# Respreading the loads, features and DMA transposes of each attention batch in a fused cosformer-attention and FFN kernel

## The chip, the cores and the metric

The kernel runs on one core of one Trainium2 chip. Its time is the device time of one execution in microseconds (us). A trace starts and ends with the first and last instruction, so its span is some 2 us shorter than the time. Runs count as slow when they are over 1.5% above the fastest of the same kernel.

## The reference

```python
B, H, S, D = 8, 8, 576, 64
def phi(x, c, s):                       # c, s: cos and sin of pi/2 * pos / S
    r = np.maximum(x, 0.0)
    return np.concatenate([r * c, r * s], axis=-1)
q_p, k_p = phi(q, cos_w, sin_w), phi(k, cos_w, sin_w)
kv  = einsum('bhsf,bhsd->bhfd', k_p, v);  z = sum(k_p, axis=2)
num = einsum('bhsf,bhfd->bhsd', q_p, kv); den = einsum('bhsf,bhf->bhs', q_p, z)[..., None] + 1e-6
x = (num / den).transpose(0, 2, 1, 3).reshape(B * S, H * D)     # 4608 tokens x 512
out = (((x @ w1) * (x @ w2)) @ w3) @ w_out
```

## The kernel before

TensorE runs a fixed program. The FFN works on 9 tiles of 512 tokens. It is cut into 232 steps: tile 0 has 40, each later tile 24, so tile t starts at step 16 + 24 t. A step is mostly four 512-column matmuls. The attention of a batch is cut into small calls hung on chosen steps. They are loads of k, v and q in two pieces each, five key features (`kf`), five value copies (`vc`), five kv products (`kv`), five query features each with its DMA transpose (`qf`), and five products, each normalized and transposed into the FFN's input xT (`nu`).

```python
def features(b, dst, src, c, cos=True, sin=True, scalar_heads=H):
    ...                                                   # cut
    nc.vector.tensor_scalar(out=dst[:R, c, :, 0:D], in0=src[:R, :, c, :], ...)           # cos half
    n = scalar_heads
    nc.scalar.activation(out=dst[:R, c, 0:n, D:F], in_=src[:R, 0:n, c, :], func=ACTF.Relu, ...)  # sin half
    if n < H:
        nc.vector.tensor_scalar(out=dst[:R, c, n:H, D:F], in0=src[:R, n:H, c, :], ...)

def prep_q(b, c):
    features(b, feat_of(b)[1], raw[b, "q"], c, scalar_heads=H if b < 3 else 6)
    if c in dma_q(b):
        nc.sync.dma_start_transpose(out=att_of(b)["qpT"][...], in_=feat[b][1][...])

def x_tr(b, c, by_vector=False):
    ...                                                   # cut
    if b >= 2 or (b == 1 and c == 3):
        nc.sync.dma_start_transpose(out=xT[t][:, :, ds(o, R)], in_=xf[rows])
        return
    ...                                                   # cut: transposes on TensorE

def plan_loads(b, when):                                  # hold_back() ties a load to its step
    for piece, s in zip([(n, half) for n in "kvq" for half in range(2)], when):
        ...                                               # cut: at(s, hold_back and load)

bases = [75, 102, 127, 153, 178]                          # steps of each batch's first product
for b, last, base in zip(range(4, B), bases, bases[1:]):
    plan_loads(b, [last + s for s in (7, 9, 11, 12, 14, 16)])
    plan(b, kf=[last + s for s in (15, 16, 17, 18, 19)],
         vc=[last + s for s in (17, 18, 19, 20, 21)],
         kv=[base + s for s in (-3, -2, -2, -1, -1)],
         qf=[last + s for s in (20, 21, 22, 23, 24)],
         nu=[base + s for s in (0, 2, 4, 6, 8)])
```

## Time and profile before

| | before |
|---|---|
| time, median | 272.53 us (271.57 to 274.71, 3 runs) |
| span of the profiled run | 269.0 us |
| TensorE busy | 245.3 us, 91% |
| TensorE waiting after 70 us | 12.4 us in six rows of the list of waits |

The page's table of 40 equal slices shows where the losses lie. A digit is the busy share, or for PEclk the granted TensorE clock, in tenths.

```profile
PE   8789999999999999979999859997999399999993
...
PEclk9999999999999999999999979999999979999998
```

TensorE is dense for the first 17 slices, up to about 114 us. Then come four dips (7, 85, 7 and 3), one for each of the batches 4 to 7. Two of them are followed by a lower clock.

### The profile page before, as it was taken

What the parts mean: (1) busy time and instruction counts of PE and PEld (TensorE: products, weight loads), DVE (VectorE), ACT (ScalarE), POOL (GpSimd) and SP (SyncE); (2) the same over time, 40 slices, a digit from 0 to 9 for tenths busy, and PEclk for the clock granted to TensorE, in tenths of its full rate; (3) what the DMA queues carried; (4) which work ended last, traced back from release to release, by engine and by line L of the source; (5) the groups of instructions that cost most, each with busy time, mean ns of one, the idle gap of its engine ahead of it and who ended that gap; (6) DMA issues with size and microseconds to landing.
All of it is one profiled execution on the core that took longest, in us unless ns stands there. A gap on an engine that the chain in (4) does not pass through costs nothing.

```text
span 269.0 us, 5058 instructions
## 1 busy us (share of the span) xinstructions
PE 245.3 (91%) x1837; PEld 131.5 (49%) x1867; DVE 145.9 (54%) x380; ACT 125.5 (47%) x270; POOL 93.5 (35%) x197
## 2 busy tenths in 40 slices
PE   8789999999999999979999859997999399999993
PEld 3487555556854454434544425444545144444442
DVE  6875735555876567238645735357556536322420
ACT  2765317766734752337335613356345513324321
POOL 7564320250423500524044404441264100969200
PEclk9999999999999999999999979999999979999998
DMA  7999999799869984995889884996799753798515
GB/s 193 185 194 203 208 208 198 100 116 145 136 107 167 140 131 78 172 181 86 156 149 166 121 160 97 171 161 116 153 147 191 81 108 72 191 309 263 182 29 127
DMA packets 83896, 41.02 MB, mean 152 GB/s; under 512 B 51488, under 2 KB 80416, under 8 KB 83872
## 3 DMA queue, kind: packets, MB, share of 16 engines
q0 software_dynamic: 35456, 27.20, 65.4%
q1 hardware_dynamic: 48256, 13.38, 29.7%
q8 instruction: 14, 0.23, 0.4%
q10 hardware_dynamic: 160, 0.13, 0.2%
q14 instruction: 10, 0.08, 0.1%
HBM read 38.80 MB, written 9.44 MB: 179 GB/s over the span
## 4 chain that ended last, share of the span: by engine, by line
PE 55%; DMA 30%; ACT 4%; issue 4%; POOL 3%; DVE 3%; ACTq 0%; POOLq 0%
PE ffnps L432 23%; PE ffnps L486 21%; DMA qs<-in_q_dram 14%; DMA w3b<-in_moe_w_dram 6%; DMA qpT<-qp 4%; PE pnum L349 4%; PE ffnps L226 3%; DMA w2b<-in_moe_w_dram 3%; DMA ks<-in_k_dram 2%; ACT asb L469 2%; ACT qp L263 1%; PE pnum L291 1%; DVE xblk L361 1%; PE pst L214 1%; DVE kvs L297 1%
## 5 line engine op out<-in xcount | busy, mean ns | idle before, releaser
L432 PE MATMUL ffnps<-xT,w2b 128*128 128x512 bf16 (+2 forms) x329 | 74.3, 348 | 2.1 <-DVE abT L473 1.8
L432 PE MATMUL ffnps<-xT,w1b 128*128 128x512 bf16 (+2 forms) x326 | 74.0, 347 | 1.4 <-ACT asb L469 0.5
L486 PE MATMUL ffnps<-w34b,abT 128*128 128x512 bf16 x270 | 68.7, 393 | 2.9 <-DVE abT L473 1.4
L473 DVE TENSOR_TENSOR abT<-asb,ffnps 128x512 bf16<-128x512 bf16 x64 | 43.7, 683 | 41.7 <-PE ffnps L432 40.0
L469 ACT CAST asb<-ffnps 128x512 bf16<-128x512 f32 x64 | 37.0, 579 | 45.2 <-PE ffnps L432 38.8
L521 POOL COPY seen<-mark 1x1 bf16<-1x1 bf16 x52 | 9.3, 179 | 112.9 <-ACT mark L519 112.9
L432 PEld LDWEIGHTS <-w1b 128*128 128x128 bf16 x336 | 31.0, 98 | 29.3 <-issue 1.6
L493 ACT COPY osb<-ffnps 128x512 f32<-128x512 f32 x35 | 20.5, 585 | 53.0 <-PE ffnps L486 47.5
L432 PEld LDWEIGHTS <-w2b 128*128 128x128 bf16 x336 | 30.6, 98 | 29.0 <-issue 2.4
L486 PEld LDWEIGHTS <-abT 128*128 128x128 bf16 x280 | 26.1, 100 | 30.9 <-issue 4.3
L263 ACT ACTIVATE qp<-qs,sinv 128x384 bf16<-128x384 bf16 (+4 forms) x40 | 24.6, 648 | 10.9 <-DMA qs<-in_q_dram 6.2
L361 DVE TENSOR_TENSOR xblk<-pnum,den 128x512 bf16<-128x512 f32 (+1 forms) x39 | 26.9, 691 | 1.6 <-DVE den L360 0.2
L263 ACT ACTIVATE kp<-ks,sinv 128x384 bf16<-128x384 bf16 (+3 forms) x35 | 21.7, 641 | 8.3 <-DMA ks<-in_k_dram 8.3
L349 PE MATMUL pnum<-kvs,qpT 128*128 128x65 bf16 x312 | 16.7, 195 | 8.9 <-DMA qpT<-qp 7.5
L349 PEld LDWEIGHTS <-qpT 128*128 128x128 bf16 x320 | 15.0, 99 | 19.8 <-issue 7.8
L283 POOL COPY va<-vs 128x512 bf16<-128x512 bf16 (+1 forms) x30 | 17.6, 627 | 17.4 <-DMA vs<-in_v_dram 12.7
L417 POOL DMA_DIRECT2D out_dram<-osb x42 | 22.3, 535 | 2.6 <-issue 2.5
L359 DVE TENSOR_SCALAR den<-pnum 128x8 f32<-128x8 f32 (+1 forms) x39 | 6.4, 165 | 26.8 <-PE pnum L349 26.7
L259 DVE TENSOR_SCALAR qp<-qs,cosv 128x512 bf16<-128x512 bf16 (+1 forms) x40 | 15.1, 387 | 7.3 <-DMA qs<-in_q_dram 7.2
L259 DVE TENSOR_SCALAR kp<-ks,cosv 128x512 bf16<-128x512 bf16 (+1 forms) x35 | 13.3, 384 | 10.0 <-DMA ks<-in_k_dram 9.9
L226 PE MATMUL ffnps<-woutb,w3T 128*128 128x512 bf16 x62 | 14.9, 379 | 0.1
L291 PEld LDWEIGHTS <-kp 128*128 128x128 bf16 x280 | 11.5, 98 | 4.4 <-PE ffnps L432 0.3
(84 smaller groups left out, 194.2 us busy)
## 6 DMA issues: line engine op xcount, KB each, us to landing
out_dram<-osb POOLq DMA_DIRECT2D x16, 256.0 KB, 4.2
out_dram<-osb POOLq DMA_DIRECT2D x24, 128.0 KB, 3.6
qs<-in_q_dram POOLq DMA_DIRECT2D x9, 256.0 KB, 6.5
ks<-in_k_dram POOLq DMA_DIRECT2D x7, 320.0 KB, 6.3
qs<-in_q_dram POOLq DMA_DIRECT2D x7, 320.0 KB, 7.7
vs<-in_v_dram POOLq DMA_DIRECT2D x7, 320.0 KB, 7.3
ks<-in_k_dram POOLq DMA_DIRECT2D x7, 256.0 KB, 6.4
vs<-in_v_dram POOLq DMA_DIRECT2D x7, 256.0 KB, 7.5
```

The lines of the kernel that those rows point to most:

```text
L226: nc.tensor.matmul(acc[:, :], lhsT=w3T[:, lc, :], rhs=woutb[:, lc, :], start=(lc == 0), stop=(lc == 7))
L259: nc.vector.tensor_scalar(out=dst[:R, c, :, 0:D], in0=src[:R, :, c, :], scalar1=0.0, scalar2=cosv[:R, at:at + 1], op0=ALU.max, op1=ALU.mult)
L263: nc.scalar.activation(out=dst[:R, c, 0:n, D:F], in_=src[:R, 0:n, c, :], func=ACTF.Relu, scale=sinv[:R, at:at + 1], bias=0.0)
L283: eng.tensor_copy(out=feat_of(b)[2][:R, c, :, 0:D], in_=raw[b, "v"][:R, :, c, :])
L349: nc.tensor.matmul(nt[:, h // 4, ds((h % 4) * 65, 65)], lhsT=qpT[:, h, ds(at, 128)], rhs=kvs[:, h, :], start=True, stop=True)
L361: nc.vector.tensor_tensor(out=xblk[rows], in0=n4[:, :, :, 0:D], in1=den[rows].unsqueeze(3).to_broadcast([R, 2, 4, D]), op=ALU.mult)
L417: on.dma_start(out=rows[:, :, cols], in_=osb[64 * i:64 * i + rows.shape[0], :, cols])
L432: nc.tensor.matmul(out, lhsT=w[:, kc, ts(jc, 128)], rhs=x[:, kc, tok], start=(kc == 0), stop=(kc == 3))
L469: nc.scalar.copy(out=asb[:], in_=aT[:, :])
L473: nc.vector.tensor_mul(out=abT[:, jc, :], in0=asb[:], in1=bT[:, :])
L486: nc.tensor.matmul(ops[:, :], lhsT=abT[:, jc, ts(ms, 128)], rhs=w34b[:, jc, :], start=(jc == 0), stop=(jc == 7))
L493: nc.scalar.copy(out=osb[:, ms % 2, :], in_=ops[:, :])
```

## The change

The intent is to use the whole cycle of a batch, about 25 steps. Loads of keys and queries go at least 9 steps ahead of their features. Query features and their transposes go 12 steps ahead of the product. Loads, features and products sit 2 to 4 steps apart, mostly 3 or 4. The order of loads becomes k, q, v, and the sin half of every feature runs whole on ScalarE.

```diff
     def prep_k(b, c):
-        features(b, feat_of(b)[0], raw[b, "k"], c, scalar_heads=H if b < 3 else 6)
+        features(b, feat_of(b)[0], raw[b, "k"], c)
     def prep_q(b, c):
-        features(b, feat_of(b)[1], raw[b, "q"], c, scalar_heads=H if b < 3 else 6)
+        features(b, feat_of(b)[1], raw[b, "q"], c)
 ...
-        for piece, s in zip([(n, half) for n in "kvq" for half in range(2)], when):
+        for piece, s in zip([(n, half) for n in "kqv" for half in range(2)], when):
 ...
-    plan_loads(3, (51, 53, 55, 57, 59, 61))
-    plan(3, kf=(59, 60, 62, 63, 65), vc=(62, 63, 64, 65, 66), kv=(72, 73, 73, 74, 74),
-         qf=(67, 69, 71, 73, 75), nu=(75, 77, 79, 81, 83))
-    bases = [75, 102, 127, 153, 178]
+    plan_loads(3, (46, 48, 51, 53, 56, 59))
+    plan(3, kf=(54, 57, 59, 61, 63), vc=(64, 65, 66, 67, 68), kv=(71, 72, 72, 73, 73),
+         qf=(60, 63, 66, 69, 72), nu=(74, 77, 80, 84, 87))
+    bases = [74, 101, 126, 152, 176]
     for b, last, base in zip(range(4, B), bases, bases[1:]):
-        plan_loads(b, [last + s for s in (7, 9, 11, 12, 14, 16)])
-        plan(b, kf=[last + s for s in (15, 16, 17, 18, 19)],
-             vc=[last + s for s in (17, 18, 19, 20, 21)],
+        plan_loads(b, [last + s for s in (-8, -5, -1, 3, 7, 11)])
+        plan(b, kf=[last + s for s in (4, 7, 10, 13, 15)],
+             vc=[base + s for s in (-10, -9, -8, -7, -6)],
              kv=[base + s for s in (-3, -2, -2, -1, -1)],
-             qf=[last + s for s in (20, 21, 22, 23, 24)],
-             nu=[base + s for s in (0, 2, 4, 6, 8)])
+             qf=[base + s for s in (-12, -9, -6, -3, 0)],
+             nu=[base + s for s in (0, 3, 6, 9, 12)])
 ...   # cut: the same loads of batch 2 in the new order; output stores some steps moved
```

More of the change, by code (lines that the diff above doesn't have):

```diff
@@ L590 @@
         at(s, lambda c=c: q_tr(1, c))
-    plan_loads(2, (27, 28, 35, 36, 31, 33))
+    plan_loads(2, (27, 28, 31, 33, 35, 36))
     plan(2, kf=(33, 35, 37, 39, 40), vc=(41, 42, 43, 44, 45), kv=(45, 46, 46, 47, 47),
          qf=(40, 41, 42, 43, 44), nu=(48, 50, 52, 54, 57))
-    plan_loads(3, (51, 53, 55, 57, 59, 61))
-    plan(3, kf=(59, 60, 62, 63, 65), vc=(62, 63, 64, 65, 66), kv=(72, 73, 73, 74, 74),
-         qf=(67, 69, 71, 73, 75), nu=(75, 77, 79, 81, 83))
-    bases = [75, 102, 127, 153, 178]
+    plan_loads(3, (46, 48, 51, 53, 56, 59))
+    plan(3, kf=(54, 57, 59, 61, 63), vc=(64, 65, 66, 67, 68), kv=(71, 72, 72, 73, 73),
+         qf=(60, 63, 66, 69, 72), nu=(74, 77, 80, 84, 87))
+    bases = [74, 101, 126, 152, 176]
     for b, last, base in zip(range(4, B), bases, bases[1:]):
-        plan_loads(b, [last + s for s in (7, 9, 11, 12, 14, 16)])
-        plan(b, kf=[last + s for s in (15, 16, 17, 18, 19)],
-             vc=[last + s for s in (17, 18, 19, 20, 21)],
+        plan_loads(b, [last + s for s in (-8, -5, -1, 3, 7, 11)])
+        plan(b, kf=[last + s for s in (4, 7, 10, 13, 15)],
+             vc=[base + s for s in (-10, -9, -8, -7, -6)],
              kv=[base + s for s in (-3, -2, -2, -1, -1)],
-             qf=[last + s for s in (20, 21, 22, 23, 24)],
-             nu=[base + s for s in (0, 2, 4, 6, 8)])
+             qf=[base + s for s in (-12, -9, -6, -3, 0)],
+             nu=[base + s for s in (0, 3, 6, 9, 12)])
     for i in range(2 * (NT - 1)):
@@ L611, in put @@
             store(nc.gpsimd, kept[i][:, :, :], 2 * i, 2)
-        at((81, 107, 132, 158)[i] if i < 4 else max(189 + 2 * (i - 4), 40 + 12 * (i - 2)), put)
+        at((88, 115, 140, 166)[i] if i < 4 else 185 + 2 * (i - 4), put)
     g = 0
```

## The prediction

> **What bounds the kernel now.** I first read the page's engine totals. TensorE is busy 245.3 of 269.0 us, VectorE 54%, ScalarE 47%. So the end can come earlier only where TensorE stands still or runs slowly. Then I asked whom TensorE's matmuls waited for, from 70 us (the second FFN tile; the change touches nothing before it) to the end.
>
> ```profile
> PE pnum L349 <- DMA qpT<-qp: 7.5, 3, 3.6
> PE ffnps L432 <- DVE abT L473: 1.8, 1, 1.8
> PE ffnps L486 <- DVE abT L473: 1.4, 1, 1.4
> PE ffnps L486 <- ACT asb L469: 0.9, 1, 0.9
> PE ffnps L432 <- ACT asb L469: 0.5, 1, 0.5
> ```
>
> Columns: us in all, times, longest. With one more row of 0.3 us (the first product waiting for the copy of kv) that is 12.4 us. The largest row is the first attention product of a batch (L349), waiting for the DMA transposes of its query features. The rows on abT and asb look like FFN evictions, but the timeline around 119 us shows what those really waited for:
>
> ```profile
> 119.04 0.61 ACT L263 ACTIVATE kp<-ks,sinv 128x384 bf16<-128x384 bf16 x1 [3.49 <-DMA ks<-in_k_dram]
> ...
> 119.47 0.68 DVE L473 TENSOR_TENSOR abT<-asb,ffnps 128x512 bf16<-128x512 bf16 x1
> ...
> 120.21 1.02 PE L432 MATMUL ffnps<-xT,w2b 128*128 128x512 bf16 x4 [1.82 <-DVE abT L473]
> ```
>
> The key features of batch 4 head the queues of ScalarE and VectorE, their load has not landed, both engines stand still (in brackets: 3.49 us on ScalarE, and 4.18 us on VectorE in a row left out), the FFN evictions behind them stand too, and TensorE runs out of PSUM tiles. So all these waits have one cause: loads are issued a few us ahead of their features, and transposes a few us ahead of their product. The chain of work that ended last agrees (start, us, what):
>
> ```profile
> 200.34 8.21 DMA qs<-in_q_dram
> 208.68 0.42 issue
> 209.10 0.47 ACT asb L469
> 209.57 1.31 ACT qp L263 x3
> 210.89 4.93 DMA qpT<-qp
> 215.87 0.62 PE pnum L349 x8
> 216.49 3.15 PE ffnps L486 x8
> 219.64 0.26 PE pnum L349 x8
> 219.90 1.73 PE ffnps L486 x8
> ```
>
> A query load takes 8.21 us, its features follow at once, their transpose takes 4.93 us and only then comes the product. The last lines show a second cost: eight output matmuls take 3.15 us right after the stall and 1.73 us later, so 1.42 us more. After the 3.56 us stall of batch 5 the same eight take 3.41 us, 1.68 more.
>
> The stretches between the first products of successive batches (3 to 4, 4 to 5, 5 to 6, 6 to 7; last 2 to 3, a well-fed cycle for comparison):
>
> ```profile
> 100.19:129.64 29.45, 26.62 (x184) 12.99 (x188) 17.52 (x48) 13.54 (x32) 8.84 (x19) 1.00 0.84 135
> 129.64:157.51 27.87, 24.10 (x176) 12.28 (x180) 16.45 (x45) 13.19 (x31) 8.86 (x19) 1.00 0.98 146
> 157.51:186.37 28.86, 27.14 (x182) 13.13 (x185) 15.57 (x44) 13.23 (x31) 10.32 (x22) 0.94 0.87 136
> 186.37:215.87 29.50, 24.47 (x177) 12.24 (x181) 16.36 (x44) 12.98 (x31) 9.37 (x20) 1.00 1.08 145
> ...
> 74.09:100.19 26.10, 25.88 (x186) 13.10 (x188) 16.55 (x44) 14.08 (x31) 8.20 (x17) 1.00 0.99 134
> ```
>
> After the window come its length, then busy us of PE, PEld, DVE, ACT, POOL, the granted clock, DMA share and GB/s. The cycle up to batch 3 (last line) is 27 program steps long (first products at steps 48 and 75) and takes 26.10 us with TensorE busy 99%. The four later ones are 27, 25, 26 and 25 steps and take 28 to 29.5 us.
>
> **What the Trainium skill says.** "TensorE: Matmul & The Clock Gate", section "Part 1: The HAM clock gate", says that TensorE falls to half clock after about 3.4 us idle and returns after a busy window as long. The trace agrees: the stalls of 3.56 and 3.41 us are followed by matmuls at about twice the time, and that of 0.53 us (batch 6) by none. So a long stall here costs about 1.5 us more than its length. The same page's specification table calls the queues of ScalarE and VectorE strict FIFO; the quoted 119 us timeline agrees. "DMA: Bandwidth & Descriptors", section "Issuing engines are not separate DMA queues", says that DMAs of all issuers share the same 16 engines and interleave. The trace agrees at least for crowding: five pieces of batch 4, issued 1 to 2 us apart, take 7.6 to 9.1 us from issue to landing, those of batch 3, 2 steps apart, 5.3 to 7.0. "Perfetto Trace Analysis", section "Identifying the Most-Contended Engine", warns that DMA occupancy misleads and that HBM use should be read: here 179 GB/s over the span.
>
> **The change, part by part.** One step is one FFN group: four 512-column matmuls, 4 x 0.216 = 0.864 us (the chain has eight in 1.73).
>
> Loads. For batches 4 to 7 the key pieces move from 7 and 9 steps after the previous batch's first product to 8 and 5 before it; their features come 4 to 15 after. That is at least 9 steps, over 8 us, from second piece to first feature, against 6 before. Queries load at -1 and 3, and their features start 12 steps before the batch's own first product, 12 to 15 after the previous one. So at least 9 steps there too. A load of 5.3 to 7.0 us is then hidden. This removes the abT and asb waits, 4.6 us.
>
> Transposes. Each chunk's transpose is now issued 12 steps ahead of its product, over 10 us, against 3.3 us from issue to landing (page, 32 transposes). The built program's waits show that the first product waits only for the transposes of its own columns (one, or two in odd batches), not for the one just issued. This removes 7.5 us and with it both slow stretches, 1.42 + 1.68 = 3.1 us.
>
> Features. Every second half of a feature now runs whole on ScalarE: 50 activations grow from 384 to 512 columns, 613 to 721 ns, so +5.4 us of ScalarE, and 50 VectorE operations of 0.25 to 0.38 us go (7.3 + 7.1 less the first batch's 0.3, 14 us). ScalarE has 13 us of work in a 29 us cycle; neither is on the path once the data is there. I count 0.
>
> Product spacing goes from 2 to 3 steps; normalizing one takes 0.18 + 0.21 + 0.70 us, inside 2 steps already. 0.
>
> Sum in two ways. By waits: 12.4 + 3.1 = 15.5 us. By pace: batch 3's cycle gives 26.10 us for 27 steps, so 24.37 for 25 and 25.24 for 26; losses 29.45 - 26.10 = 3.35, 27.87 - 24.37 = 3.50, 28.86 - 25.24 = 3.62, 29.50 - 24.37 = 5.13, sum 15.6 (this includes batch 5's slow stretch), plus the tail's 1.42: 17.0 us. The pace also counts gaps too short for the list of waits; I take it. Full success: 272.5 - 17.0 = 255.5 us.
>
> **Rivals.** *GpSimd's value copies become the late link.* Values now load last, second piece at 11 steps after the previous first product, and kv products start 21 to 24 after it. Landing in 7.0 us (7.2 steps of 0.967 us), plus 0.5 us of mark and issue, puts the data at about step 18.7; four copies of 0.63 us and, on the same queue, the next key load with its mark (1.1 us) end at 22.4. The last kv products come at step 23 to 26, and batch 7, with only 23, has no next key load. A margin of 1 to 3 steps; at 9.1 us landing, the worst piece seen, it would be gone in some batches and cost about 0.5 us each, at most 2 in all. I charge 1.5 us for this and other small new waits. *DMA becomes the bound.* A cycle moves about 135 GB/s x 29.45 us = 4.0 MB; in 25 us that is 160 GB/s. Five-us stretches of loads with transposes reach 195 to 202, the tail's stores 305, so I estimate enough room, and 10 us of lead absorbs slower transposes. Were each cycle held at 27 us by it, the gain would halve: about 264. *Transposes are slower among loads*, so that products still wait; speaking for it, those of x take 5.1 to 6.7 us in crowded stretches against 3.3 alone. Even 6.7 fits in 10. *ScalarE's longer features delay the FFN evictions*: 0.1 us each against a rotation of four PSUM tiles; under 1 us in all.
>
> **Range and chances.** 255.5 + 1.5 = 257.0 us. Below: everything hidden and a run like the fastest of before (271.57), 254 and a little less. Above: half of the gain lost to DMA crowding, 264. Range 253 to 263. 2% faster is 267.1 us; to miss it two thirds of the stalls would have to come back. Faster 0.95, same 0.04, slower 0.01.
>
> **What would show it.** In the changed profile: no wait of L349 for qpT over 0.5 us; ScalarE and VectorE hardly wait for ks and qs (before 14.5 and 17.1 us, a small part of it in the unchanged start); the four cycles at 0.97 to 1.0 us per step; granted clock near 1.00 after 70 us; the chain almost only matmuls from 100 us on, no DMA of qs. What would make it wrong: kv products (L291) waiting for GpSimd's va; load landings over 9 us everywhere and feature waits of the old size; or a PSUM wait on evictions behind the longer activations.

## The result, and the profile after

The changed kernel took 259.33 us (median; 257.85 to 262.3 in 4 runs, of which the one at 262.3 counts as slow) beside 272.84 us for the kernel before (4 runs). The ratio of the fast runs is 0.948, 95% interval 0.940 to 0.957. Ratios here are the mean time of one kernel's fast runs over that of the other's of the same rounds, so they are not quite the ratio of the medians. The span went from 269.0 to 256.0 us.

The waits of TensorE's matmuls from 70 us on (us in all, times, longest), which were six rows and 12.4 us before, are now two rows:

```profile
PE ffnps L432 <- DMA xT<-xblk: 2.8, 2, 1.5
PE ffnps L432 <- ACT osb L493: 0.9, 1, 0.9
```

All the old waits are gone: qpT, abT, asb and the copy of kv. A wait stands there that the list of before did not have after 70 us. The first matmul of an FFN tile waits for a DMA transpose of the attention output; the two of the first row are tile 2 at 89.8 us and tile 6 at 186.0 us. The second row is the same case: it is the first matmul of tile 5, at 161.06 us, the last transpose that it needs landed at 160.96 us, and in a repeat of this kernel that place is listed as a wait for xT.

The cycles, from first product to first product, in the columns of the prediction's table (window, length, busy us of PE, PEld, DVE, ACT, POOL, then clock, DMA share, GB/s):

```profile
74.16:100.78 26.62, 25.18 (x182) 12.67 (x185) 14.75 (x35) 14.71 (x33) 9.05 (x20) 1.00 1.39 149
100.78:126.87 26.09, 25.82 (x185) 13.12 (x189) 15.05 (x35) 14.95 (x32) 8.78 (x19) 1.00 1.25 159
126.87:151.23 24.36, 24.14 (x177) 12.32 (x180) 15.32 (x36) 13.42 (x31) 8.69 (x19) 1.00 1.19 162
151.23:177.49 26.26, 25.13 (x181) 12.80 (x185) 14.39 (x36) 15.04 (x32) 10.20 (x22) 1.00 1.14 151
177.49:202.71 25.22, 23.45 (x173) 11.86 (x176) 15.01 (x35) 13.88 (x28) 7.41 (x15) 1.00 1.12 158
```

The first line is the cycle of 26 steps up to batch 3. It held 27 steps before, and took 26.10 us then. The next four hold 27, 25, 26 and 24 steps. They took 29.45, 27.87, 28.86 and 29.50 us for 27, 25, 26 and 25 steps. Two things can be read here. The cycles to batches 4 and 5 run at 0.97 us per step, the pace that was foretold for all. The other three lost 1 us or more each: TensorE is busy only 25.18 of 26.62 us in the first line, for instance. The clock is 1.00 everywhere.

The chain of work that ended last, from 179 us on (start, us, what), answers to the chain of before:

```profile
179.10 6.86 DMA xT<-xblk
186.01 1.90 PE ffnps L432 x8
187.91 0.26 PE pnum L349 x8
188.17 2.59 PE ffnps L432 x12
...
202.71 0.42 PE pnum L349 x8
203.13 2.59 PE ffnps L486 x12
```

No load and no qpT is in it any more. The first product of batch 7 (202.71) follows other TensorE work and the copy of kv without a stall, and the matmuls behind it run at full speed (12 in 2.59 us). What is left in this stretch is a transpose of x that took 6.86 us.

Why are transposes of x late? The list of DMA issues gives medians from issue to landing. Before:

```profile
qpT<-qp SPq DMA_TRANSPOSE x32, 3.3
xT<-xblk SPq DMA_TRANSPOSE x31, 3.2
```

After:

```profile
qpT<-qp SPq DMA_TRANSPOSE x32, 5.1
xT<-xblk SPq DMA_TRANSPOSE x31, 4.7
```

The same transposes take half as long again now that more loads run beside them, the longest of x 10.4 us in place of 7.4. That loads are the cause is tested by run 9 below.

### The profile page after: what moved, and what is told of

The parts are those of the page before. It is cut to its first block, busy times and chain, and to the rows that moved or that the text cites. A ratio compares the mean times of both kernels' runs of the same rounds, so it can differ in the third digit from the quotient of the medians.

```text
span 256.0 us, 5013 instructions
## 1 busy us (share of the span) xinstructions
PE 241.5 (94%) x1837; PEld 131.3 (51%) x1867; DVE 137.6 (54%) x330; ACT 131.2 (51%) x270; POOL 92.8 (36%) x197
## 4 chain that ended last, share of the span: by engine, by line
PE 80%; DMA 10%; DVE 3%; ACT 3%; issue 2%; POOL 1%; ACTq 0%; POOLq 0%
PE ffnps L432 46%; PE ffnps L486 17%; DMA xT<-xblk 7%; PE ffnps L226 5%; PE pnum L349 4%; PE pnum L291 3%; DMA qs<-in_q_dram 3%; PE pst L214 1%; DVE kvs L297 1%; DVE xblk L361 1%; PE pst L322 1%; ACT kvs L296 1%; PE pst L387 1%; ACT osb L493 0%; POOL vs L125 0%
## 5 line engine op out<-in xcount | busy, mean ns | idle before, releaser
L486 PE MATMUL ffnps<-w34b,abT 128*128 128x512 bf16 x270 | 64.1, 379 | 0.5
L263 ACT ACTIVATE qp<-qs,sinv 128x512 bf16<-128x512 bf16 (+2 forms) x40 | 28.0, 715 | 1.7 <-DMA qs<-in_q_dram 1.7
L263 ACT ACTIVATE kp<-ks,sinv 128x512 bf16<-128x512 bf16 (+1 forms) x35 | 24.9, 718 | 0.6 <-DMA ks<-in_k_dram 0.5
L259 DVE TENSOR_SCALAR qp<-qs,cosv 128x512 bf16<-128x512 bf16 (+1 forms) x40 | 17.7, 453 | 3.5 <-DMA qs<-in_q_dram 3.4
L291 PEld LDWEIGHTS <-kp 128*128 128x128 bf16 x280 | 11.5, 98 | 4.1
L291 PE MATMUL pnum<-va,kp 128*128 128x65 bf16 x280 | 12.2, 194 | 0.0
## 6 DMA issues: line engine op xcount, KB each, us to landing
out_dram<-osb POOLq DMA_DIRECT2D x16, 256.0 KB, 5.1
qs<-in_q_dram POOLq DMA_DIRECT2D x9, 256.0 KB, 8.4
ks<-in_k_dram POOLq DMA_DIRECT2D x7, 256.0 KB, 7.7
vs<-in_v_dram POOLq DMA_DIRECT2D x7, 256.0 KB, 4.7
```

Source lines behind the costliest of these rows:

```text
L291: nc.tensor.matmul(kvt[:, h // 4, ds((h % 4) * 65, 65)], lhsT=kp[:, c, h, :], rhs=va[:, c, h, 0:D + 1], start=(i == 0 and h % 4 == 0), sto ...
L486: nc.tensor.matmul(ops[:, :], lhsT=abT[:, jc, ts(ms, 128)], rhs=w34b[:, jc, :], start=(jc == 0), stop=(jc == 7))
```

## The experiments

Twelve more runs were made, one of them (e10) the changed kernel again. All gave correct results. My theory was at first that the lead of the loads is nearly all of the gain.

**1. Early loads alone (e3).** The kernel before, with only the loads moved.

```diff
-        plan_loads(b, [last + s for s in (7, 9, 11, 12, 14, 16)])      # order k, v, q
+        plan_loads(b, [last + s for s in (-4, -2, 0, 3, 7, 11)])       # order k, q, v
```

> The kernel before with one part of the change alone: for batches 4 to 7 the loads are issued at steps -4, -2 (keys), 0, 3 (queries), 7, 11 (values) after the previous first product; all features, transposes and products stay bunched at the old steps. Theory (the late loads cause nearly everything; transposes then start at their planned 5 to 7 steps before the product and need about 3.3 to 5 us): no wait of the product for qpT over 0.7 us, abT and asb waits gone, clock near 1.00, time 256 to 261 us. Rival (the transposes' own 12 steps of lead are needed): waits for qpT stay at 1 to 3 us per batch, time 264 to 269 us.

Measured: 289.12 us (287.73 to 290.7, all fast), ratio 1.0625, interval 1.055 to 1.070. Both the theory and the rival fell. The early loads alone make the kernel 6% slower. TensorE's waits in this run, from 95 us on:

```profile
PE pnum L349 <- DMA qpT<-qp: 15.3, 8, 4.5
PE ffnps L432 <- DMA xT<-xblk: 8.7, 2, 5.6
```

The waits on abT and asb are gone, as foretold, so loads no longer hold up the features. But the transposes are now the stall. The chain of this run shows how long single ones take:

```profile
101.33 8.30 DMA qpT<-qp
...
132.67 11.54 DMA xT<-xblk
144.21 0.14 issue
144.34 12.76 PE ffnps L432 x52
```

In the kernel before, the transposes of batches 4 to 7 lie from 7 steps before the first product to 8 after it, and loads are issued 7 to 16 steps after it. Most transposes meet no load. Those of x that do are slow there too: four of batch 2's five, beside the loads of batch 3, took 6.5 to 7.4 us. Early loads lie on top of the transposes, which start only 5 to 7 steps before the first product. So the two parts of the change can't be added up: the loads' lead costs 17 us without the transposes' lead.

**2. The rest that the first needed (e9).** The same kernel, with the query features and their transposes 12 to 8 steps ahead as well.

```diff
-             qf=[last + s for s in (20, 21, 22, 23, 24)],
+             qf=[base + s for s in (-12, -11, -10, -9, -8)],
```

> The kernel with early loads alone (289.1 us) plus one more part of the change for batches 4 to 7: query features and their transposes 12 to 8 steps before the first product, one step apart; x transposes still 2 steps apart, key features and the feature split still old. Theory formed after that run (early loads lie on top of the transposes, which then land in 5 to 11 us; only their 12 steps of lead make that harmless): the 15.3 us of waits for qpT and the slow matmuls after them go, waits for xT of a few us may remain, 262 to 270 us. Rival (the early loads harm in another way, for example by the order of the queue of GpSimd or by key loads at -4 and -2): still over 278 us.

Measured: 262.16 us (258.79 to 266.55), ratio of the two fast runs 0.952, interval 0.946 to 0.958. That is 27 us less than run 1, by this line alone. In the profiled run TensorE waits for qpT once, 0.9 us. So the revised theory holds: early loads and early transposes together make the gain. The key features are still bunched here, the products still 2 steps apart and the feature split still the old one; the output stores and the first products, which the change moves by some steps, stand at their old steps too. Yet the two fast runs (258.79 and 258.96 us) stand where the whole change stands. The other two runs, at 265 and 267 us, count as slow; I come back to this spread.

**3. Query features late again (e4).** The whole change, with `qf` moved back.

```diff
-             qf=[base + s for s in (-12, -9, -6, -3, 0)],
+             qf=[base + s for s in (-5, -4, -3, -2, -1)],
```

> The changed kernel with the query features and their transposes of batches 4 to 7 moved back to 5 to 1 steps before the first product (loads stay early). Theory (load lead is what counts): within 2 us of the changed kernel, about 258 to 261 us, waits for qpT at most 0.5 us per batch. Rival (transpose lead counts): a wait of 1.5 to 3.5 us before each of the four first products, 264 to 270 us.

Measured: 265.41 us median, but one run at 260.47 and three at 264.7 to 267.9, which leaves one fast run. The profile is of the fast one:

```profile
PE pnum L349 <- DMA qpT<-qp: 4.1, 3, 1.9
```

The waits of the product for qpT come back, though smaller than in run 1. The sign is the rival's: the transposes' lead matters. By the rule of 2% the verdict is unclear, and the size stays open between 1 and 9 us, since only the fast run has a profile.

**4. Bunched, with the leads kept (e5).** Is it the spacing of 3 to 4 steps that helps?

```diff
-        plan(b, kf=[last + s for s in (4, 7, 10, 13, 15)],
+        plan(b, kf=[last + s for s in (4, 5, 6, 7, 8)],
-             qf=[base + s for s in (-12, -9, -6, -3, 0)],
-             nu=[base + s for s in (0, 3, 6, 9, 12)])
+             qf=[base + s for s in (-12, -11, -10, -9, -8)],
+             nu=[base + s for s in (0, 2, 4, 6, 8)])
```

> The changed kernel with its leads kept but its spacing taken away for batches 4 to 7: key features at last+4 to +8 and query features with transposes at base-12 to base-8, one step apart, products 2 steps apart. Theory (lead, not spacing): within 1.5 us of the changed kernel, 257 to 260 us; perhaps faster where the x transposes come earlier. Rival (spacing keeps the queues of ScalarE and VectorE free for evictions): abT and asb waits of 1 us or more per batch, over 263 us.

Measured: 257.23 us (255.42 to 258.67, all fast), ratio 0.945, interval 0.938 to 0.952. Without the spacing of features and products the kernel is as fast, if anything faster. It is the lead that pays and not this spreading. The loads kept their spacing here; in run 9 four of the six stand 2 steps apart, and nothing is lost. Waits for xT in the profile of this run are one of 0.3 us. Tile 5's last block is produced one step earlier here. Tile 6's comes at the same step as in the change, and its transpose took 5.9 us in place of 6.9; no run shows why.

**5. Filling two stalls (e7).** The kernel before, with useless work on TensorE where it stood before the first products of batches 5 and 7.

```diff
+        if b in (5, 7):
+            at(base, lambda: filler(48))      # 48 transposes of zeros into a spare PSUM tile
```

> The kernel before with 48 useless 128-column transposes (about 2.7 us) put on TensorE just before the first products of batches 5 and 7, where it stood 3.4 to 3.6 us. Theory (the idle stretch itself throws the clock down afterwards): the stalls get no longer, the eight output matmuls after them take 1.73 us in place of 3.41 and 3.15, time about 3 us less, 269 to 270 us. Rival (the slow matmuls have another cause, or only queue behind something): same time as before or up to 3 us longer, 272 to 275 us.

Measured: 267.54 us (266.81 to 267.84), ratio 0.983, interval 0.977 to 0.988 (below 2%, so by rule unclear, but clear of 1): more work, and 4.4 us less. The chain after the first filler (start, us, what):

```profile
156.74 0.42 PE pnum L349 x8
157.16 1.73 PE ffnps L486 x8
158.89 0.26 PE pnum L349 x8
159.14 1.73 PE ffnps L486 x8
```

The first eight matmuls after the product take 1.73 us, where the same place took 3.41 us before; those after the second filler are as fast. The mean granted clock is 0.99 to 1.00 in place of 0.98. So it is the standing still that makes the following matmuls slow: with TensorE kept at work in the same place they are fast. This accounts for 3.1 us; where the other 1.3 us comes from I did not find.

**6 and 7. The feature split (e1, e2).** First the change without it, then it alone.

```diff
-        features(b, feat_of(b)[0], raw[b, "k"], c)                                          # e1; q alike
+        features(b, feat_of(b)[0], raw[b, "k"], c, scalar_heads=H if b < 3 else 6)
```

> The changed kernel with the old split of the feature halves (6 heads on ScalarE, 2 on VectorE from batch 3 on). Theory (neither engine is on the path once the data is there): 0 within 1 us, 258 to 260 us; ScalarE busy about 5 us less, VectorE about 12 us more. Rival (relief of VectorE was a part of the gain): 2 us or more slower, over 261 us.

Measured: 262.21 us median, two fast runs (257.68 and 261.3) and four between 261.9 and 262.8 that count as slow; ratio 0.954, interval 0.947 to 0.962. The profile that I have is of a slow run and shows 5.1 us of waits for xT, 3.7 us of them at tile 5, with a granted clock of 0.50 for the 3.4 us from then on. About the split this was inconclusive.

```diff
-        features(b, feat_of(b)[0], raw[b, "k"], c, scalar_heads=H if b < 3 else 6)          # e2; q alike
+        features(b, feat_of(b)[0], raw[b, "k"], c)
```

> The kernel before with only the split of the feature halves changed (all 8 heads on ScalarE). Theory: same within 1.5 us, 271 to 274 us, because features there wait for loads and not for the engines; late features get 0.1 us longer each, so if anything slightly slower. Rival (relief of VectorE): 268 to 270 us.

Measured: 271.31 us (270.52 to 272.4), ratio 0.998, interval 0.993 to 1.003. Alone, the split does nothing.

**8. Two blocks of x transposed on TensorE (e6).**

```diff
-        if b >= 2 or (b == 1 and c == 3):
+        if (b >= 2 and (b, c) not in ((3, 1), (6, 0))) or (b == 1 and c == 3):      # both 2 steps later
```

> The changed kernel with the two attention blocks on whose DMA transposes the FFN tiles 3 and 6 waited (batch 3 block 0 of step 80, batch 6 block 0 of step 152) transposed on TensorE instead, 2 steps after their product. Theory (slow DMA transposes among loads are the new wait): the waits for xT of 1.2 and 1.5 us go, about 2 to 2.8 us less, 256 to 257 us. Rival (the wait only moves, to another block of the same tile or to the evictions): within 0.7 us of the changed kernel.

Measured: 258.05 us (255.34 to 259.25, the longest slow), ratio 0.946, interval 0.941 to 0.951. Half of this was aimed badly. Tile 6, which waited 1.54 us, no longer waits. But the wait at 89.8 us that I had put down to tile 3 belongs to tile 2: step 64 runs at 89.8 us, and the block it needs is block 2 of batch 2, produced at step 52. That one I had left alone. So this run shows only that the cure works where it was applied; tile 5 (0.85 us) and tile 2 (0.28 us) still waited.

**9. Queries loaded later (e8).**

```diff
-        plan_loads(b, [last + s for s in (-8, -5, -1, 3, 7, 11)])
+        plan_loads(b, [last + s for s in (-8, -5, 5, 7, 9, 11)])
```

> The changed kernel with the query loads of batches 4 to 7 moved from steps -1 and 3 to 5 and 7, and the last value piece from 11 to 11 with the first at 9. Theory (the x transposes are slowed by the query loads in flight beside them): the x transpose of batch 6 lands in about 4 us in place of 6.9 and tile 6's wait of 1.5 us goes; tile 3's transpose, at step 80, then stands between query and value loads and stays slow; total 0.5 to 1.5 us less unless query features wait. Rival (transposes are slow because of their own queue): the landing stays 6 to 7 us and so does the wait.

Measured: 255.11 us (254.79 to 257.75, all fast), ratio 0.940, interval 0.936 to 0.944. That is some 4 us below the change (259.33 us, in other rounds), more than the 0.5 to 1.5 us foretold. With the query loads moved off the steps just around the first product, the waits of tiles 5 and 6 go. The only listed wait after 70 us is again that of tile 2, at 89.68 us:

```profile
89.68 1.02 PE L432 MATMUL ffnps<-xT,w1b 128*128 128x512 bf16 x4 [1.43 <-ACT qp L263]
```

The bracket names an activation, but this matmul reads only xT and w1b. It is the same wait as in the change's own profile, where the bracket says xT. The loads beside tile 2's transposes are those of batch 3, which this run leaves in place. So where the loads were moved the wait went, and where they stayed it stayed. Single transposes say the same. The block that tile 5 waited for landed in 2.5 us here and in 5.3 in the change, that of tile 6 in 4.2 and in 6.9, and tile 2's, with the old loads beside it, in 10.0 and in 9.8. The three last blocks of batch 6, which now have the query loads beside them, went the other way, from 2.4 to 3.4 us to 5.6 to 6.2. The transposes of x as a whole, in the change and in this run:

```profile
DMA to landing us min/median/max: 2.3/4.7/10.4
DMA to landing us min/median/max: 2.4/5.3/10.0
```

The median rose while the waits went. So loads beside the transposes make them late, and the cure was not fewer late ones but that the late ones have more time. The expectation's reason for the second half named the wrong tile, as in run 8.

**10 to 12. The change again, the two cures together, and the split once more (e10, e11, e12),** five rounds each on one chip.

```diff
-        if b >= 2 or (b == 1 and c == 3):                              # e11: run 9's loads, and
+        if (b >= 2 and (b, c) != (2, 2)) or (b == 1 and c == 3):       # tile 2's block on TensorE at step 54
```

> The changed kernel itself, in the same rounds as the next two, since its times spread (257.9 to 262.3 in four runs): 258 to 260 us median, waits of the FFN tiles for xT of 1 to 4 us that differ from run to run.

> The changed kernel with the queries loaded at 5 and 7 (as in the run with later queries, 255.1 us) and the one x block on which FFN tile 2 really waited (batch 2, block 2, produced at step 52, not a block of batch 3 as I had written for the earlier runs) transposed on TensorE two steps later. Theory: tile 2's wait of 1.4 us goes and nothing takes its place, 253.5 to 254.5 us. Rival: the wait moves to another block of tile 2, 255 us.

> The kernel of the run before with the old split of the feature halves (6 heads on ScalarE, 2 on VectorE from batch 3 on), where no waits for transposes blur the comparison. Theory (the split is worth nothing): within 0.7 us of that run. Rival (the longer VectorE work delays normalization and so the x transposes, as the one profile of the first such run with 5.1 us of waits for xT suggests): 1 to 3 us slower.

| run | median (range), us | ratio of fast runs (interval) |
|---|---|---|
| e10, the change | 259.54 (258.33 to 262.96, the longest slow) | 0.953 (0.949 to 0.957) |
| e11, both cures | 253.80 (253.66 to 255.63) | 0.935 (0.931 to 0.939) |
| e12, e11 with 6 heads | 254.05 (253.37 to 255.08) | 0.935 (0.931 to 0.939) |

The table's medians take in the slow run. In the profile of e10 the waits for xT are 4.2 us in three places, tiles 2, 5 and 6. In e12's there is no listed wait of TensorE after 70 us. The profile of e11 fell on its slowest run and shows one wait of 1.2 us, of a kv product for a value copy of GpSimd. e11 beats both kernels: 5.7 us below the change, 18 us below the kernel before. The difference between e11 and e12 is 0.25 us, so the split of the features is worth nothing that these runs can tell, and the longer runs of run 6 are best put down to waits for xT. Where the transposes have lead enough, the runs also agree with each other better: e11 and e12 spread over 2 us, the change over 4 to 5, and e4 and e9 over 7 to 8. I take the spread for collisions of loads and transposes that fall differently from run to run. One slow run was profiled, that of run 6, and it agrees: two transposes of x that took 7.2 and 6.2 us, a wait of 3.7 us for them and slow matmuls after it. For the other slow runs this is not shown.

## Why the prediction was right, point by point

The time on record was 257.0 us with a range of 253 to 263; 259.33 us lies in it, and the verdict, faster by 5.2%, is the one that was given 0.95.

- **The bound and the removed waits: right.** The 12.4 us of waits after 70 us went, all rows of them. For ks and qs ScalarE and VectorE waited 12.4 and 16.1 us after 70 us; 0.5 and 3.2 us are left.
- **The clock: right.** The 3.1 us of slow matmuls are gone, the clock is 1.00, and run 5 shows that the standing still was their cause.
- **Features and split: 0, right.** Run 7 and the pair of runs 11 and 12 measure it.
- **"Transposes are slower among loads", "Even 6.7 fits in 10": the step that failed.** The rival was named and then checked for qpT alone. The x transposes have a deadline too, the first step of the next FFN tile that needs them, and the prediction did not look at it. The size was too small as well: the trace of before already had x transposes of up to 7.4 us, and now they take up to 10.4. The block of tile 5 (7 steps ahead of the tile) landed in 5.3 us where it had taken 2.5, that of tile 6 (8 steps) in 6.9 in place of 2.5, that of tile 2 (12 steps) in 9.8 in place of 6.9. Tile 6, for instance, came up 7.0 us after its block's product; the transpose was issued 1.6 us after that product and took 6.9. The waits of the three tiles cost 2.8 + 0.9 = 3.7 us in the profile, 4.2 in the repeat.
- **Product spacing: 0, right.** It would be easy to blame the 3 steps between products, but they took no lead from the blocks that were late: in the kernel before these came 7, 7 and 12 steps ahead of tiles 5, 6 and 2, in the changed one 7, 8 and 12.
- **The allowance: mis-sized and in the wrong place.** I charged 1.5 us, mainly for GpSimd's value copies. In this profile no kv product waits for them (in the slowest run of e11 one does, 1.2 us); new waits took 3.7 us. That is most of the way from 257.0 to 259.33. The sum closes: 17.0 us foretold, less 3.7, makes 13.3 us, and the spans differ by 13.0.
- **Loads 4.6 us and transposes 7.5 us: right together, not one by one.** The prediction lists them as two gains and does not say that the first needs the second. Run 1 measured the first alone at 17 us slower, run 2 both at once.
- **The signs: two missed.** The cycles to batches 6 and 7 took 1.01 and 1.05 us per step where 0.97 to 1.0 was foretold, and the chain after 100 us still has the transpose of x of 6.86 us.
- **The rival "DMA becomes the bound": not seen as a bound.** The cycles move 149 to 162 GB/s at full pace, as estimated (160). But DMA crowding showed as latency: transposes of 5 us and more where 3.3 was the median.

## What to carry to other kernels

Moving a load earlier is not free. Look at what else uses the DMA engines at the new time, above all transfers with a short deadline such as DMA transposes, and give those more lead first or place the loads where none of them is under way. Check the deadline of every consumer of a transfer that the change could slow down, not only of the one that waits now. When many small transfers must share a stretch, their lead in front of their use counts; spacing features and products evenly brought nothing here.

## What the Trainium skill lacked or had wrong

- "DMA: Bandwidth & Descriptors", section "Rules for kernel authors", says: "A transpose next to ordinary DMAs needs nothing". That is about correct data. I found nothing on the page on how long a transpose takes from issue to landing among loads. Here the median is 3.2 to 3.3 us where few loads and transposes meet, 4.7 to 5.1 us where they share the time, and 11.5 us at worst. For time, a transpose next to ordinary DMAs needs lead.
- "TensorE: Matmul & The Clock Gate", section "Part 1: The HAM clock gate", puts the idle window at about 3.4 us. In run 1 a single stall of 2.57 us (before 232.99 us) was already followed by eight matmuls in 2.92 us in place of 1.73, and the granted clock was 0.50 from 232.5 to 235.8 us, although TensorE had been busy for 1.41 of the 3.4 us before; stalls of 1.59 and 1.37 us were not followed by slow ones.
- The same page, section "Part 4: PE-mode transpose", says that transposes on TensorE do not count as busy in the same way for the clock. In run 5, 48 of them (2.84 us) in a gap of about 3.1 us kept the clock at full speed. Beside the stall of 2.57 us above, which lost it, this suggests that they do count here. But the trace lists them as matmuls of zeros and does not tell whether they ran in the page's transpose mode, and no run was made to settle it.
